# Turning half of a tile by DMA instead of TensorE, with token halves and a value load in two parts

## The chip, the cores and the metric

One core of one Trainium2 chip. The metric is device microseconds of one execution. Kernels are compared only within the same rounds. The profile is one execution, and its span (first to last instruction) is some 2 us under the time of the run.

## The reference

```python
kv = einsum('bhsd,bhse->bhde', k, v)            # 8 batches, 8 heads, 576 tokens, 64 wide
out = einsum('bhsd,bhde->bhse', q, kv)
out = out / sqrt(mean(out*out, -1) + 1e-6) * g_norm
x = out.transpose(0, 2, 1, 3).reshape(4608, 512)
xn = x / sqrt(mean(x*x, -1) + 1e-6) * rms_g     # then a gated feed-forward layer
g = xn @ w_gate                                 # 512 -> 1536
return (g * sigmoid(g) * (xn @ w_val)) @ w_out  # 1536 -> 512
```

## The kernel before

The kernel works through batches of 512 tokens (the 64 left over of each batch make a ninth). While TensorE runs the feed-forward of batch n, the other engines prepare batch n+1 and DMA loads n+2. A feed-forward has 12 *units*, each the gate and value products of 128 columns, and then 4 *down products*. The weights stand still in the array and the tokens move, so the normalised rows must first be turned: tokens along the free dimension (`xnt`). From batch 2 on DMA turns them. Batch 1 is turned by TensorE, four groups of four matmuls against an identity (the profile merges them into two of eight), and copied out of PSUM:

```python
def to_rows(x, n, c, ps, engine):
    for j in range(NS):
        PE.matmul(ps[:, j, :], lhsT=x[:, 2 * j : 2 * j + 2, :], rhs=identity, is_transpose=True, ...)
    cast(engine, xnts[n][:, :, 128 * c : 128 * c + 128], ps)
...
def load_batch(b):                    # queries, keys, values of one batch on the sync queue
    load_q(b)
    for name in ("k", "v"):
        alloc_kv(b, name)
        load_kv(b, name, nc.sync)
...
xs = [F.scale(c, F.outa[c]) for c in range(4)]     # batch 1's rows, VectorE
alloc_q(2)
for i in range(T):
    cast_q(2, i, SC if i < 2 else DVE)
for c in range(T):
    atts[2].q_rows(c)                 # batch 2's queries turned by DMA, sync queue
down_part(1, 8, 12)
f_x(0, xs[0], SC)                     # to_rows through TensorE
f_x(1, xs[1], SC)
down_part(2, 8, 12)
f_x(2, xs[2], DVE)
f_x(3, xs[3], DVE)
down_part(3, 8, 12)
for c in range(T):
    ffn.down_out(c)                   # batch 0's output, stored on the sync queue
```

Then the units of batch 1, with the work for batches 2 and 3 hung on them as steps:

```python
def up(self, j):                      # one unit: 8 matmuls of 512 tokens
    ...
def up_pair(self, i, lo, banks=None): # two units, 256 tokens: 16 matmuls of 256 tokens
    ...
steps[0] += [cast_kv(2, "v", i, GP) for i in (0, 1)]     # n == 1, cut
steps[1] += [cast_kv(2, "v", i, DVE) for i in (2, 3)]
steps[2] += [a.kv_products, a.kv_copy]                   # L289: key-value products of batch 2
steps[4] += [a.o_products]                               # L329: query products
...
for c in range(T):
    steps[13].append(lambda b=b, c=c: atts[b].q_rows(c)) # query turns of batch n + 2
```

Every engine takes its instructions in order, so a TensorE instruction that waits holds back all that follow (in the trace after, products of L289 waited 0.68 us until 60.06, and the pair of units behind them began only at 60.83).

## Time and profile before

| | before |
|---|---|
| time, median of the first 3 runs | 318.66 us (318.55 to 318.67) |
| span in the profile | 316.9 us |
| TensorE busy | 97% |
| VectorE, ScalarE busy | 57%, 56% |
| 16 KB instruction packets on queue 8 | 18 |

Read it from TensorE: where its row has no hole, only its own work counts. The lines of this are in the prediction below.

### The profile page before, as it was taken

What the parts mean: (1) busy time and instruction counts of PE and PEld (TensorE: products, weight loads), DVE (VectorE), ACT (ScalarE), POOL (GpSimd) and SP (SyncE); (2) the same over time, 40 slices, a digit from 0 to 9 for tenths busy, and PEclk for the clock granted to TensorE, in tenths of its full rate; (3) what the DMA queues carried; (4) which work ended last, traced back from release to release, by engine and by line L of the source; (5) the groups of instructions that cost most, each with busy time, mean ns of one, the idle gap of its engine ahead of it and who ended that gap; (6) DMA issues with size and microseconds to landing.
All of it is one profiled execution on the core that took longest, in us unless ns stands there. A gap on an engine that the chain in (4) does not pass through costs nothing.

```text
span 316.9 us, 6002 instructions
## 1 busy us (share of the span) xinstructions
PE 307.4 (97%) x2334; PEld 150.1 (47%) x2371; DVE 180.4 (57%) x377; ACT 176.5 (56%) x326; POOL 22.7 (7%) x48
## 2 busy tenths in 40 slices
PE   7899999999999999999999999999999999999995
PEld 3585455444444444444444444444444444444443
DVE  3676658679339913992289327941795079504310
ACT  3677458385667565746683668376844274233321
POOL 2364351100000000000000000000000000000000
PEclk9999999999999999999999999999999999999999
DMA  7999999587479157906790589838003710330014
GB/s 264 378 387 387 375 374 337 122 229 269 117 173 375 41 146 191 360 2 133 186 375 4 116 167 220 330 73 188 8 0 66 153 48 3 63 135 3 0 33 100
DMA packets 60316, 54.95 MB, mean 173 GB/s; under 512 B 36348, under 2 KB 44800, under 8 KB 60288
## 3 DMA queue, kind: packets, MB, share of 16 engines
q1 hardware_dynamic: 59776, 53.85, 56.6%
q10 hardware_dynamic: 448, 0.72, 0.7%
q8 instruction: 18, 0.29, 0.4%
q14 instruction: 10, 0.08, 0.1%
q0 software_dynamic: 64, 0.00, 0.0%
HBM read 37.75 MB, written 9.44 MB: 149 GB/s over the span
## 4 chain that ended last, share of the span: by engine, by line
PE 90%; DMA 5%; another core or an unknown queue 1%; issue 1%; SPq 1%; POOL 1%; DVE 0%; ACT 0%
PE v_ps L497 29%; PE g_ps L497 28%; PE o_ps L549 26%; DMA st<-in_moe_w_val_dram 3%; DMA st<-in_k_dram 2%; PE att_ps L289 2%; PE g_ps L549 1%; PE v_ps L549 1%; DMA out_dram<-o_sb 1%; PE att_ps L329 1%; PE o_ps L514 1%; POOL wv_sb L194 1%; PE o_ps L329 0%; PE att_ps L265 0%
## 5 line engine op out<-in xcount | busy, mean ns | idle before, releaser
L503 DVE TENSOR_TENSOR h_sb<-silu,v_ps 128x512 bf16<-128x512 bf16 x104 | 71.2, 684 | 100.1 <-ACT silu L502 68.5
L497 PE MATMUL v_ps<-xnt,wv_sb 128*128 128x512 bf16 x409 | 106.2, 379 | 0.7
L497 PE MATMUL g_ps<-xnt,wg_sb 128*128 128x512 bf16 x398 | 104.6, 379 | 0.7
L502 ACT ACTIVATE silu<-g_ps 128x512 bf16<-128x512 f32 x104 | 62.1, 597 | 70.2 <-PE g_ps L497 57.4
L549 PE MATMUL o_ps<-wo_sb,h_sb 128*128 128x512 bf16 x386 | 86.8, 379 | 0.4
L497 PEld LDWEIGHTS <-wv_sb 128*128 128x128 bf16 x416 | 40.7, 98 | 49.1
L549 PEld LDWEIGHTS <-h_sb 128*128 128x128 bf16 x420 | 40.6, 98 | 47.6 <-issue 0.4
L497 PEld LDWEIGHTS <-wg_sb 128*128 128x128 bf16 x416 | 39.5, 98 | 46.4
L105 ACT COPY o_sb<-o_ps 128x512 f32<-128x512 f32 (+1 forms) x34 | 19.6, 581 | 40.2 <-PE o_ps L549 36.6
L105 ACT CAST vb<-st 128x576 bf16<-128x576 f32 (+1 forms) x26 | 16.1, 662 | 3.7 <-DMA st<-in_v_dram 3.7
L376 DVE TENSOR_TENSOR xna<-outa,s1y 128x512 bf16<-128x512 bf16 x28 | 17.9, 684 | 0.0
L105 ACT CAST qb<-st 128x512 bf16<-128x512 f32 (+1 forms) x30 | 16.2, 602 | 2.3 <-DMA st<-in_q_dram 2.1
L359 DVE TENSOR_REDUCE ssq<-sqt 128x16 f32<-128x1024 bf16 x14 | 17.1, 1220 | 0.5
L359 DVE TENSOR_REDUCE ssq<-sq 128x16 f32<-128x1024 bf16 x14 | 17.1, 1220 | 0.5
L105 ACT CAST kb<-st 128x576 bf16<-128x576 f32 x20 | 12.5, 673 | 0.0
L344 ACT ACTIVATE sq<-att_ps 128x512 bf16<-128x512 f32 x14 | 7.6, 594 | 4.3 <-PE att_ps L329 3.6
L358 DVE TENSOR_TENSOR sq<-sq,gsq 128x512 bf16<-128x512 bf16 x14 | 5.9, 422 | 4.9 <-ACT sq L344 4.9
L107 DVE CAST kb<-st 128x576 bf16<-128x576 f32 x12 | 6.0, 518 | 4.2 <-DMA st<-in_k_dram 4.2
L649 PE MATMUL att_ps<-kv_all 128*128 128x512 bf16 (+1 forms) x21 | 7.1, 461 | 1.2 <-DVE sel L637 1.2
L107 POOL CAST wo_sb<-st 128x512 bf16<-128x512 f32 x12 | 7.3, 635 | 7.4 <-DMA st<-in_moe_w_out_dram 7.4
L344 ACT ACTIVATE sqt<-o_ps 128x512 bf16<-128x512 f32 x14 | 7.6, 597 | 0.0
L350 ACT CAST outa<-o_ps 128x512 bf16<-128x512 f32 x14 | 7.5, 591 | 0.0
(153 smaller groups left out, 182.1 us busy)
## 6 DMA issues: line engine op xcount, KB each, us to landing
st<-in_k_dram SPq DMA_DIRECT2D x7, 1152.0 KB, 10.1
st<-in_v_dram SPq DMA_DIRECT2D x7, 1152.0 KB, 11.7
out_dram<-o_sb SPq DMA_DIRECT2D x14, 512.0 KB, 3.0
st<-in_q_dram SPq DMA_DIRECT2D x6, 1024.0 KB, 6.7
st<-in_moe_w_out_dram SPq DMA_DIRECT2D x6, 512.0 KB, 10.4
st<-in_moe_w_gate_dram SPq DMA_DIRECT2D x4, 512.0 KB, 9.0
st<-in_moe_w_val_dram SPq DMA_DIRECT2D x4, 512.0 KB, 10.9
out_dram<-o_sb SPq DMA_DIRECT2D x14, 128.0 KB, 2.4
```

The lines of the kernel that those rows point to most:

```text
L105: engine.copy(out=dst, in_=src)
L107: engine.tensor_copy(out=dst, in_=src)
L289: PE.matmul(self.kv_ps[x][to, a, :], lhsT=kb[rows, 2 * a + x, c, :], rhs=vb[rows, 2 * a + x, c, :], start=(a == 0 and c == 0), stop=(a == ...
L344: SC.activation(out=self.in_place(self.sq[i][:, 0], g), in_=bank, func=ACT.Square)
L350: SC.copy(out=self.in_place(rows, g), in_=bank)
L359: DVE.reduce_sum(out=self.ssq[:, c], in_=sq, axis=AX.X)
L376: DVE.tensor_tensor(out=self.xna[c], in0=self.outa[c], in1=self.alpha[:, c, :].to_broadcast([128, H, D]), op=OP.mult)
L497: PE.matmul(ps, lhsT=wt[:, s, j * 128 : (j + 1) * 128], rhs=x[:, s, :], start=(s == 0), stop=(s == NS - 1),)
L502: SC.activation(out=silu, in_=g_ps, func=ACT.Silu)
L503: DVE.tensor_tensor(out=self.h[:, j, :], in0=silu, in1=v_ps, op=OP.mult)
L549: PE.matmul(self.o_ps[c], lhsT=self.h[:, j, c * 128 : (c + 1) * 128], rhs=wo_sb[:, j, :], start=(j == 0), stop=(j == NF - 1),)
L649: PE.matmul(ps[:, 0:w], lhsT=warm_sb[:, 0:128], rhs=warm_sb[:, 0:w], start=True, stop=True, skip_group_check=True)
```

## The change

Its intent: take the turns of token columns 2 and 3 off TensorE (8 matmuls and 2 copies) and give them to DMA. They land later than TensorE's would have, so the first four units run in halves: two pairs on the first 256 tokens, then two pairs on the rest. And so that the turns are not held up behind batch 2's values, half of those values is loaded after them.

```diff
-    def load_batch(b):
+    def load_batch(b, first=slice(0, NS)):
         load_q(b)
-        for name in ("k", "v"):
+        for name, js in (("k", slice(0, NS)), ("v", first)):
             alloc_kv(b, name)
-            load_kv(b, name, nc.sync)
+            load_kv(b, name, nc.sync, js)
...
-    load_batch(2)
+    load_batch(2, slice(0, 2))
...
     atts = {b: Att(b) for b in range(2, B + 1)}
+    for c in (2, 3):
+        nc.sync.dma_start_transpose(
+            out=xnts[1][:, :, 128 * c : 128 * c + 128], in_=xs[c].rearrange("p h d -> p (h d)")
+        )
+    load_kv(2, "v", nc.sync, slice(2, 4))
     for c in range(T):
         atts[2].q_rows(c)
...
-    f_x(2, xs[2], DVE)
-    f_x(3, xs[3], DVE)
...
-            if unit < NF:
+            if n == 1 and unit < 4:
+                i, lo = unit % 2, 256 * (unit // 2)
+                ffn.gate_pair(i, lo, ffn.up_pair(i, lo))
+            elif unit < NF:
                 ffn.up(unit)
```

## The prediction

> **What bounds the kernel now.** I read the page's table of busy shares first, then the chain of work that ended last, then the stretch that the change touches. The page says which engine to count on:
>
> ```profile
> PE 307.4 (97%) x2334; PEld 150.1 (47%) x2371; DVE 180.4 (57%) x377; ACT 176.5 (56%) x326; POOL 22.7 (7%) x48
> PE 90%; DMA 5%; another core or an unknown queue 1%; issue 1%; SPq 1%; POOL 1%; DVE 0%; ACT 0%
> ```
>
> The second line is the chain by engine. TensorE is busy for 97% of the span and carries 90% of the chain; the 5% of DMA is the opening load of batch 0 and the last store. VectorE and ScalarE work for little more than half of the span. So a change is worth what it takes off TensorE's own row of work, or adds to it as a wait, and hardly anything else.
>
> The change lies between the last down products of batch 0 and the first units of batch 1. The chain cut to 50 to 61 us (start, duration, what) shows it piece by piece:
>
> ```profile
> 50.28 1.73 PE o_ps L549 x8
> 52.00 0.45 PE att_ps L265 x8
> 52.45 0.86 PE g_ps L549 x4
> 53.31 0.46 PE att_ps L265 x8
> 53.77 0.86 PE v_ps L549 x4
> 54.63 0.22 PE g_ps L497
> 54.85 0.05 issue
> ...
> 58.95 0.86 PE v_ps L497 x4
> 59.81 0.71 PE att_ps L289 x72
> ```
>
> There is no hole: each piece starts where the one before ended. The two groups of L265 are the turns of batch 1's normalised rows through TensorE: eight small matmuls for token columns 0 and 1, eight for columns 2 and 3. From 54.63 on the units of batch 1 run, 1.73 us each (0.86 gate, 0.86 value), and at 59.81, after the third unit, stand the key-value products of batch 2.
>
> What the sync queue and VectorE do in these microseconds, from the timeline of each:
>
> ```profile
> 53.69 5.23 SPq L303 DMA_TRANSPOSE qt<-qb  x4
> 59.03 6.57 SPq L569 DMA_DIRECT2D out_dram<-o_sb  x8
> ```
> ```profile
> 52.19 0.68 DVE L478 TENSOR_TENSOR xna<-outa,F1y 128x512 bf16<-128x512 bf16 x1
> 52.79 0.75 DVE L107 CAST qb<-st 128x512 bf16<-128x512 f32 x2
> 53.58 0.76 DVE L107 COPY xnt<-att_ps 128x512 bf16<-128x512 bf16 x2
> ...
> 58.20 0.69 DVE L503 TENSOR_TENSOR h_sb<-silu,v_ps 128x512 bf16<-128x512 bf16 x1
> 58.80 0.82 DVE L107 CAST vb<-st 128x576 bf16<-128x576 f32 x2
> ```
>
> The last of the four scaled rows is ready at 52.87. The second copy out of PSUM ends at 54.34, 0.29 us before TensorE's first unit. The casts of batch 2's values for heads' groups 2 and 3 end at 59.62, 0.19 us before the products that read them. That second margin is thin, and the change touches it.
>
> **What the Trainium skill says.** "TensorE: Matmul & The Clock Gate", Part 4: PE-mode transpose, gives about 275 ns for one transpose in a kernel's context, and a copy out of PSUM after it. The trace has 216 to 219 ns as the duration of one, but the chain charges 0.46 us for eight, because they are pipelined; I use 0.46. The same page, Back-to-back issue gap, has 262 cycles for 256 columns and 518 for 512 (109 and 216 ns at its 2.4 GHz), so halving costs almost nothing provided that the weight load fits under the shorter matmul. The trace agrees: L514, batch 0's units in halves, has groups of 8 in 0.87 us (0.109 each), L497 has 4 in 0.86, and a weight load takes 98 ns, under 109. "DMA: Bandwidth & Descriptors", Queues, rings and completion order: descriptors of one queue are consumed in ring order on each DMA engine. So a turn issued behind a load waits for that load's packets. The trace has the first of the four query turns, issued at 53.69 behind the tail of the value load, at 2.9 us to landing, the rest at 2.5. "Perfetto Trace Analysis", DMA Instruction, HWDGE: the shown time of a DMA instruction is descriptor generation, not movement. Here one turn holds the sync queue for 1.27 us and lands 2.5 us after its start, so four in a row are paced by issue.
>
> **The change part by part.**
>
> (a) *Removed from TensorE:* the second group of L265, 0.46 us in the chain. Removed from VectorE: two copies of about 0.42 us; VectorE has room, so this counts for nothing. First unit: 54.63 - 0.46 = 54.17.
>
> (b) *Added to TensorE by the halves:* four units of 8 matmuls of 512 columns (4 x 1.73 = 6.91 us) become 64 matmuls of 256 columns: 64 x 0.1085 = 6.94. Cost 0.03 us. ScalarE and VectorE still do 4 activations and 4 products, each of 2 x 256 columns, the size of before.
>
> (c) *The two turns on the sync queue.* The third scaled row is ready about 52.25, the fourth at 52.87; add about 0.14 us for the wait (79.90 against 79.76 for the same hand-over in the next batch). First turn: issued 52.39, off the queue 53.65; second: 53.65 to 54.92. With 2.5 us to landing, and up to 0.4 more for packets ahead of them, the second lands at 56.15 to 56.55. With the halves, TensorE needs token columns 2 and 3 only after two pairs, at 54.17 + 2 x 1.735 = 57.64. More than 1 us to spare: these turns are hidden.
>
> (d) *The value load in two.* Before, the load's packets (2304 bytes) flow at full rate until about 53.8, stragglers to 55.4, and it lands at 56.0 to 56.2. Half of 1152 KB taken out is 576 KB, at about 380 GB/s (page, GB/s row) 1.5 us: first half down at about 54.5, before its user needs it, and the ring is nearly clear when the turns arrive. The second half is issued when the turns are off the queue, at about 54.95. Packets of loads issued into an empty ring start some 1.2 us after (59.03 issue, 60.2 first store packet). So 56.15 + 1.55 = 57.7 for the last packet, and some 0.5 to 1 us of receipt and stragglers: landing at 58.2 to 58.7.
>
> (e) *The products that wait for it.* VectorE's casts follow unit 1's product, which comes 0.44 us earlier than before: free at about 58.4. Casts take 0.82 to 0.90, so they end at 59.3 to 59.6; TensorE finishes its third unit at 54.17 + 3 x 1.735 = 59.38 and needs some 0.1 us after the cast. Wait: 0.05 to 0.35 us, my middle is 0.2.
>
> (f) *Later on the queue.* Query turns: from about 55.45, last landing at 55.45 + 3 x 1.27 + 2.5 = 61.8; their matmuls stand at about 63.6. Stores and the next batch's loads move back by 1.6 us; the next batch's first cast stands at 76.5 and its load was issued at 65.69 and took some 7 us. All keep their slack.
>
> Sum: -0.46 + 0.03 + 0.20 = -0.23 us. As TensorE runs without a hole to the end, a shift here passes to the end: 318.66 - 0.23 = 318.4.
>
> **The rivals.**
>
> *The wait replaces the turns' time.* If the second value half lands at 59.0 or later (slow DMA engines lag, or the query turns behind it interleave), casts end after 59.9 and TensorE waits over 0.5 us: time back at 318.7 or, at 59.5, 319.2. For it: the thin margin of 0.19 us before, and a load that now starts after two turns. Against: the load is only 576 KB in a nearly empty ring.
>
> *The full gain.* If the half lands by 58.3, the wait is nothing and the time is 318.66 - 0.43 = 318.2. For it: my landing estimate has its early edge there.
>
> *Coarse waiting.* If the first unit's matmuls wait for both turns, not for their own half of the tile, they start at 56.2 to 56.6, some 2 us late: 320.3. Against: batch 0 already starts its units on the first 256 tokens while the rest are being turned.
>
> *TensorE becomes bound by weight loads in the halves.* 64 loads of 98 ns are 6.27 us, under 6.94. It would show as over 0.12 us a matmul; the trace's L514 speaks against it.
>
> **Range and chances.** The terms run from -0.43 (no wait) to about +0.2 (a wait of 0.65); three runs of before spread over 0.12 us. That gives 318.1 to 318.9, widened to 317.9 to 319.0 for what I left out. Two per cent is 6.4 us: no term is near it, even coarse waiting is 1.7 us. So "within 2%" is almost certain.
>
> **What would show it.** (a) One group of L265 left in the chain, and the first unit at about 54.2. (b) Groups of 8 half matmuls at 0.87 us each. (c) Two more turns on the sync queue from about 52.4; no hole in TensorE's row before the third pair. (d, e) The value load's second half landing at 58.2 to 58.7; a hole of 0.05 to 0.35 us before the products of L289. (f) No wait at the query products. The prediction is wrong if that hole is over 0.6 us, if the turns land after 57.6, or if a later load, moved back, opens a hole in the next batch.

## The result, and the profile after

The changed kernel took 320.24 us (median of 6 fast runs, 319.97 to 320.9), the kernel before 318.75 us (6 fast runs, 318.55 to 319.48). The ratio is 1.0045, 95% interval 1.0031 to 1.0059. A ratio here is the mean time of one kernel's fast runs over that of the other's of the same rounds, so not quite the ratio of the medians quoted. Within 2%, as foretold; but 1.5 us slower instead of 0.2 us faster, and outside the range.

The page of the changed kernel, busy shares and the chain by engine:

```profile
PE 307.9 (97%) x2359; PEld 152.9 (48%) x2395; DVE 179.3 (56%) x375; ACT 176.3 (55%) x326; POOL 22.7 (7%) x48
PE 84%; DMA 8%; DVE 2%; SPq 2%; issue 1%; another core or an unknown queue 1%; POOL 1%; ACT 0%; DVEq 0%
```

The busy share did not move, but TensorE's share of the chain fell from 90% to 84%. That alone does not show a new wait: e9 below, which has none here, stands at 85%, because its chain goes through loads in the opening. What TensorE itself waited for, in total us, times, longest:

```profile
PE o_ps L329 <- DMA qt<-qb: 0.7, 1, 0.7
PE att_ps L671 <- ACT qb L105: 0.7, 1, 0.7
PE att_ps L289 <- DVE vb L107: 0.7, 1, 0.7
```

The middle line is in the opening, and was there before (0.9). The other two are new. The chain of the changed kernel from 50 to 61 us (this trace runs 0.45 us ahead of that of before: the first scaled row is taken up at 49.86 against 50.31; the operation itself starts 0.06 us later):

```profile
53.84 1.13 SPq L968
54.97 0.05 issue
55.03 4.50 DMA st<-in_v_dram
59.52 0.02 issue
59.55 0.04 DVE vb L107
59.58 0.34 issue
59.92 0.46 DVE vb L107
60.38 0.04 issue
60.43 0.47 PE att_ps L289 x34
```

The chain has left TensorE. It goes through the second half of the values (issued at 55.03, landed 59.52), VectorE's two casts of it, and only then comes back to TensorE, in the middle of the key-value products. The sync queue and VectorE in the same stretch:

```profile
51.85 3.12 SPq L968 DMA_TRANSPOSE xnt<-xna  x2
55.03 0.58 SPq L120 DMA_DIRECT2D st<-in_v_dram  x1
55.78 5.11 SPq L303 DMA_TRANSPOSE qt<-qb  x4
```
```profile
59.55 0.83 DVE L107 CAST vb<-st 128x576 bf16<-128x576 f32 x2 [1.53 <-DMA st<-in_v_dram]
```

VectorE stood idle for 1.53 us until the load had landed. Before, it went straight from unit 1's product to these casts, at 58.80.

The second new wait comes one batch later. The chain there:

```profile
90.56 4.23 DMA qt<-qb
94.80 0.05 issue
94.84 0.29 PE o_ps L329 x8
```

The last of batch 3's four query turns took 4.23 us to land, where 2.5 is usual. Before, there was no wait at the same place:

```profile
93.20 0.34 PE att_ps L329 x16
93.54 0.23 PE o_ps L329 x16
```

**Three measures that do not depend on the opening.** The opening varies between runs by more than the change is worth, so I measure in each trace (a) how long TensorE takes from the end of the work before the products of L289 to their end, (b) the same for the query products of L329 in batch 3, (c) the stretch from when the first scaled row of batch 1 (the first L478) is taken up to the last instruction. Each is of one profiled execution. All three are worked out from the starts and ends of the instructions in the trace.

| run | (a) L289 | (b) L329 | (c) scaled row to end | (c) minus that of before |
|---|---|---|---|---|
| before | 0.71 | 0.57 | 266.63 | |
| after | 1.93 | 1.49 | 268.27 | +1.64 |
| e1 values whole | 0.71 | 0.57 | 266.21 | -0.42 |
| e2 halves only | 0.71 | 1.30 | 267.45 | +0.82 |
| e3 before, 48 instructions more | 0.70 | 1.69 | 267.89 | +1.26 |
| e5 values whole, earlier query turns | 0.71 | 0.57 | 266.15 | -0.48 |
| e6 after, earlier query turns | 1.37 | 0.57 | 266.97 | +0.34 |
| e7 three quarters ahead | 0.70 | 1.48 | 267.15 | +0.52 |
| e8 = e1 again | 0.71 | 1.31 | 266.99 | +0.36 |
| e9 = e5 again | 0.71 | 0.57 | 266.19 | -0.44 |
| e10 before, earlier query turns | 0.71 | 0.57 | 266.67 | +0.04 |
| e11 after again | 1.18 | 1.62 | 267.63 | +1.00 |

For after: (a) grew by 1.22, (b) by 0.92, together 2.14; less the 0.46 of the turns that makes 1.68, against 1.64 measured. For e11: 0.47 + 1.05 - 0.46 = 1.06 against 1.00. So two waits account for the loss, and the saving is there beneath them.

### The profile page after: what moved, and what is told of

Same layout as the page of the kernel before. It is cut to its first block, busy times and chain, and to the rows that moved or that the text cites. A ratio compares the mean times of both kernels' runs of the same rounds, so it can differ in the third digit from the quotient of the medians.

```text
span 318.1 us, 6055 instructions
## 1 busy us (share of the span) xinstructions
PE 307.9 (97%) x2359; PEld 152.9 (48%) x2395; DVE 179.3 (56%) x375; ACT 176.3 (55%) x326; POOL 22.7 (7%) x48
## 4 chain that ended last, share of the span: by engine, by line
PE 84%; DMA 8%; DVE 2%; SPq 2%; issue 1%; another core or an unknown queue 1%; POOL 1%; ACT 0%; DVEq 0%
PE v_ps L497 27%; PE g_ps L497 26%; PE o_ps L549 25%; DMA st<-in_moe_w_val_dram 3%; DMA st<-in_k_dram 2%; DMA st<-in_v_dram 1%; DMA qt<-qb 1%; PE att_ps L289 1%; SPq L303 1%; DVE xna L478 1%; DMA out_dram<-o_sb 1%; PE o_ps L514 1%; PE g_ps L514 1%; POOL wv_sb L194 1%
## 5 line engine op out<-in xcount | busy, mean ns | idle before, releaser
L503 DVE TENSOR_TENSOR h_sb<-silu,v_ps 128x512 bf16<-128x512 bf16 x100 | 68.4, 684 | 98.1 <-ACT silu L502 68.3
L497 PE MATMUL v_ps<-xnt,wv_sb 128*128 128x512 bf16 x393 | 102.0, 379 | 0.6
L497 PE MATMUL g_ps<-xnt,wg_sb 128*128 128x512 bf16 x383 | 100.6, 379 | 0.6
L502 ACT ACTIVATE silu<-g_ps 128x512 bf16<-128x512 f32 x100 | 59.7, 597 | 68.4 <-PE g_ps L497 55.5
L497 PEld LDWEIGHTS <-wv_sb 128*128 128x128 bf16 x400 | 39.1, 98 | 47.2
L497 PEld LDWEIGHTS <-wg_sb 128*128 128x128 bf16 x400 | 38.1, 98 | 44.5
L105 ACT CAST kv_all<-att_ps 64x128 bf16<-64x128 f32 x14 | 3.6, 259 | 7.2 <-PE att_ps L289 7.1
```

The costliest lines, as they stand in the source:

```text
L105: engine.copy(out=dst, in_=src)
L497: PE.matmul(ps, lhsT=wt[:, s, j * 128 : (j + 1) * 128], rhs=x[:, s, :], start=(s == 0), stop=(s == NS - 1),)
L502: SC.activation(out=silu, in_=g_ps, func=ACT.Silu)
L503: DVE.tensor_tensor(out=self.h[:, j, :], in0=silu, in1=v_ps, op=OP.mult)
```

## The experiments

The theory: first, the second half of the values comes too late for L289; second, a fetch of TensorE's own instructions slows the last query turn of batch 3 (the trace shows a 16 KB packet of the kind "instruction" on queue 8 at 92.44 us, while that turn is in flight, and 15 of its 16 arrivals are in by 93.04 but the sixteenth at 94.80). The rivals: the turns themselves are late; the turns behind the load slow it; the second wait is just the sync queue pushed back.

**e1, values whole again**

```diff
-    load_batch(2, slice(0, 2))
+    load_batch(2)
...
-    load_kv(2, "v", nc.sync, slice(2, 4))
```

> The changed kernel with batch 2's values loaded whole, ahead of the two turns, as before; turns and token halves stay. Theory (TensorE lost 1.4 us because the second half of the values was issued at 55.0 and landed at 59.5): the values land near 56, the wait before the products of L289 goes, the turns land near 56.6 against a need at 57.6, so 1.4 us less than the changed kernel, about 318.8; if the late last query turn of batch 3 (0.7 us) also stays. Rival (the turns need the shorter load ahead of them, as the change's author took it): the turns come behind the whole load, land after 57.6 and the third pair of token halves waits 0.5 us or more; 319.5 or more.

Measured: 319.65 us (6 runs, 318.35 to 321.49) against 319.31 (11 runs, 318.74 to 319.93) of before, ratio 1.0015, interval 0.9991 to 1.0038: not to be told apart. This chip spread the kernel before over 1.2 us in 11 runs (the runs of the result above spread over 0.9 in 6), about as much as the effects looked for. The profile is clear, though: the two turns land at 56.28 and 56.67 behind the whole load, no unit waits, (a) is back at 0.71 and (c) is 0.42 us under before. The rival falls: the turns did not need the load cut. That profile also lacked the second wait, which the theory had left open.

**e8, the same kernel again**

> e1 again, beside e5, because its profile had no wait while most of its timed runs were slower. Theory: the fetch lands within 0.2 us of the last query turn's landing, so some runs pay the wait at L329 and some not: fastest run 0.4 us under before's fastest, slower ones up to 0.9 us over. Rival: noise of that chip alone, the same ratio as e5.

Measured: 319.68 us (6 runs, 319.12 to 320.51) against 319.31 of before, ratio 1.0016, interval 1.0001 to 1.0032. This time the profile has the wait at L329 (the last turn landed at 94.12 instead of some 92.6) and (c) is +0.36. So one kernel has it in one profile and not in another. Its fastest run was not under that of before (318.74), a miss.

**e2, halves alone**

```diff
 # the kernel before, with only this of the change
-            if unit < NF:
+            if n == 1 and unit < 4:
+                i, lo = unit % 2, 256 * (unit // 2)
+                ffn.gate_pair(i, lo, ffn.up_pair(i, lo))
+            elif unit < NF:
```

> The kernel before with the four units in token halves alone; turns through TensorE, values whole. Cost of the halves themselves by the chain: 64 x 0.1085 against 32 x 0.216, 0.03 us. Theory of the second wait (a 16 KB fetch of TensorE's instructions occupies one DMA engine just when the last query turn of batch 3 is in flight): this kernel has 64 more TensorE instructions than before, 16 more than the changed one, so the fetch comes at about the same place and the wait of up to 0.7 us at the products of L329 near 94 us appears here too: 318.8 to 319.4. Rival (that wait comes from turns and stores pushed back on the sync queue): nothing is pushed back here, no wait, 318.7.

Measured: 319.92 us (6 runs, 319.56 to 321.37) against 319.31, ratio 1.0026, interval 1.0008 to 1.0044. The median is over the span that I gave; the profiled run's opening was 1.4 us longer than before's (first scaled row at 51.68). Nothing of the values or the sync queue differs from before here, and still:

```profile
PE o_ps L329 <- DMA qt<-qb: 0.6, 1, 0.6
```

(b) grew by 0.73 and (c) by 0.82, so the halves themselves cost 0.09 at most. The rival that needs a pushed-back queue falls.

**e3, the kernel before with more TensorE instructions and nothing else**

```diff
-    warm(warm_ps, 9)
+    warm(warm_ps, 33, 140)
```

> The kernel before with its first 9 warm-up matmuls of 512 columns as 33 of 140: the same columns in the idle opening, 48 more TensorE instructions, as many as the changed kernel has; nothing else. Theory of the fetch: the fetch moves earlier by 48 instructions and falls into the flight of batch 3's last query turn; one of its 16 arrivals comes some 1.8 us after the others, TensorE waits about 0.7 us before L329 near 94 us; time 0.5 to 0.8 us over before. Rival (pushed-back queue): no wait there, time of before within 0.2 us.

Measured: 320.05 us (6 runs, 318.82 to 320.63) against 319.31, ratio 1.0017, interval 0.9999 to 1.0035. The chain and TensorE's waits in its profile:

```profile
89.93 4.44 DMA qt<-qb
94.36 0.05 issue
94.41 0.29 PE o_ps L329 x8
```
```profile
PE o_ps L329 <- DMA qt<-qb: 0.9, 1, 0.9
```

The interval of the times still holds no change; the profile carries the reading. The wait is there in a kernel that differs from before only in its warm-up at the very start, 33 small matmuls for 9 large ones. So more TensorE instructions ahead are enough to bring it, with nothing else moved (one profile; e2 is a second). Where the fetch fell, from the packets and arrivals in the traces of all runs:

| run | instruction packet starts | 15th arrival of the last turn | 16th arrival | late by |
|---|---|---|---|---|
| before | 93.52 | 92.55 | 92.56 | 0.0 |
| after | 92.44 | 93.04 | 94.80 | 1.8 |
| e2 | 93.56 | 94.08 | 95.62 | 1.5 |
| e3 | 92.38 | 92.41 | 94.37 | 2.0 |
| e4 | 96.01 | 96.54 | 98.46 | 1.9 |
| e7 | 91.44 | 92.05 | 93.80 | 1.7 |
| e8 | 92.01 | 92.60 | 94.12 | 1.5 |
| e11 | 92.49 | 93.10 | 94.98 | 1.9 |
| e1 | 92.04 | 92.18 | 92.19 | 0.0 |
| e6 | 92.15 | 92.21 | 92.22 | 0.0 |
| e5 | 93.34 | 91.54 | 91.55 | 0.0 |
| e9 | 92.89 | 91.79 | 91.80 | 0.0 |
| e10 | 93.50 | 91.56 | 91.57 | 0.0 |

Where the packet starts after the turn has landed, nothing is late; where it starts half a microsecond before the 15th arrival, one arrival is late. Close to the end it goes either way (e3 late at 0.03 us, e1 and e6 not at 0.14 and 0.06). The packets in the traces tell why. The turn's packets end with 32 of 4 bytes. In all seven late rows thirty of these start in time, and the last two start within 0.02 us of the end of the instruction packet (after: 93.75 and 93.76 against 93.77), 0.7 to 1.2 us behind the other thirty. In e1 and e6 all 32 had started (the last at 91.87 and 91.89) before the instruction packet did; in e3 two had not. So the late share stood behind the instruction packet.

That the packet is TensorE's instruction stream is inferred, from two counts. The pages have 18 such packets in the two kernels with 2371 weight loads of TensorE (before and e10), and 19 in all those with 2395 or 2403:

```profile
q8 instruction: 18, 0.29, 0.4%
q8 instruction: 19, 0.31, 0.4%
```

And the packets keep step with TensorE: the eighth of them starts when 967 weight loads have begun in before and e10, and 973 to 975 in every other run, though the times differ by several us (107.2 to 112.8).

**e4, nothing behind the second half of the values**

```diff
-        cast_q(2, i, SC if i < 2 else DVE)
+        if i < 3:
+            cast_q(2, i, SC if i < 2 else DVE)
...
-    for c in range(T):
-        atts[2].q_rows(c)
...
+            steps[1] += [lambda: cast_q(2, 3, DVE)]
+            steps[1] += [lambda c=c: atts[2].q_rows(c) for c in range(T)]
 # and batch 0's stores after these (cut)
```

> The changed kernel, but nothing follows the second half of the values on the sync queue for some 2.5 us: batch 2's query turns wait for a cast placed after the second pair, and batch 0's stores come after them. Its time is not of interest (the query products may wait). Theory (a load starts slowly by itself: its first 1.5 us move a quarter of the later rate): the second half still takes 4.3 to 4.5 us from issue to landing. Rival (the query turns issued straight behind it slow it): it takes 3.4 us or less.

Measured (one look, 323.91 us, as the query products now wait): 55.13 to 59.18, 4.05 us, between the two. The turns behind the load cost 0.2 to 0.45 us (4.26, 4.32 and 4.49 in e11, e6 and after); most of the lateness is the load's own.

**e7, a quarter behind instead of a half**

```diff
-    load_batch(2, slice(0, 2))
+    load_batch(2, slice(0, 3))
-    load_kv(2, "v", nc.sync, slice(2, 4))
+    load_kv(2, "v", nc.sync, slice(3, 4))
```

> The changed kernel with three quarters of the values ahead of the turns and one quarter (288 KB) behind. Question: how much of the 4.49 us from issue to landing of the 576 KB is fixed. My prediction took 2.0 us fixed and 1.5 us of transfer at full rate, so 2.7 to 2.9 us for 288 KB and no wait at L289. Theory of the slow start (the first 2 us move only some 300 KB whatever the size): 3.5 us or more, and a wait at L289 of 0.3 to 0.8 us stays.

Measured (one look): 3.07 us from issue to landing, and no wait at L289. My theory of a fixed slow start of 3.5 us or more is wrong. Against the same queue order with 576 KB (4.26 to 4.49), the second 288 KB cost 1.2 to 1.4 us, where 380 GB/s would make it 0.78; what does not scale is 1.65 to 1.9 us, about what the prediction allowed. So it is the transfer that was mis-sized. The packets of the load show it directly: the 576 KB ran for 2.49 to 2.85 us in e4, e11, e6 and after, the 288 KB here for 1.52, which is 190 to 240 GB/s; ahead of them stand 1.18 to 1.23 us from issue to the first packet, and after them 0.35 to 0.41 to the landing. And they show how: counted from its first packet, the load of after moved 56 KB in the first 0.5 us, then 63, 83, 196 and 162, while the loads from 50 to 52 us moved 182 to 191 KB in each such slice. e4 has the same climb (52, 83, 180, 202) with nothing behind the load, so the turns behind do not make it. Why a load climbs slowly I did not settle.

**e6, the changed kernel with batch 3's query turns one unit sooner**

```diff
-                steps[13].append(lambda b=b, c=c: atts[b].q_rows(c))
+                steps[12 if n == 1 else 13].append(lambda b=b, c=c: atts[b].q_rows(c))
```

> The changed kernel with the earlier query turns of batch 3 alone; the values stay in two loads. Theory: the wait at L329 goes or shrinks below 0.3 us, the one at L289 stays; the stretch from the first scaled row to the end falls from 268.3 by some 1.0 us to 267.2; time 0.6 us over before. Rival (the wait at L329 follows from the later stores and loads and moves with them): about the changed kernel, 1.5 us over before.

Measured: 319.29 us (5 runs, 319.2 to 319.5) against 319.31, ratio 1.0002, interval 0.999 to 1.0014. (b) is back at 0.57, (a) is 1.37, (c) 266.97, 1.3 us under after (whose profile is of other rounds). The time that I expected, 0.6 us over before, did not show. The second wait goes alone, with the first left in place: they are two causes.

**e5, both waits taken away: e1 with the edit of e6**

> The changed kernel with both waits taken away: values whole as in e1, and batch 3's query turns issued one unit sooner, ahead of batch 1's first store, so that the last turn has landed about 0.6 us earlier and the instruction fetch finds the store in flight. Theory: no wait at L289 nor at L329; from the first scaled row of batch 1 to the end 266.2 us in the profile against 266.6 before; time 0.4 us under before of the same rounds (ratio 0.9987). Rival (something else than these two waits holds the changed kernel back): time of before or over.

Measured: 318.62 us (6 runs, 318.48 to 320.36), ratio 0.9995, interval 0.9975 to 1.0015. In the profile (a) and (b) are as before and (c) is 0.48 us shorter, as expected; the timed gain is not shown.

**e9, e5 again; e10, the control; e11, after again** (one other chip, same rounds)

> e5 again, because its interval (0.9975 to 1.0015) was too wide for a gain of 0.4 us. Theory: no wait at L289 or L329, stretch from the first scaled row of batch 1 to the end 266.2 us against 266.6 before; ratio 0.9985 to 0.9990. Rival (the gain is lost in other places that the profile of one run does not show): ratio 1.000 or more.

> Control: the kernel before with the earlier query turns of batch 3 alone. Theory: there was no wait to remove, so the time of before, ratio 0.9995 to 1.0005. Rival (e5 gains by the earlier query turns and not by the turns taken off TensorE): as e5.

> The changed kernel unaltered, on the chip of e9 and e10, for comparison: both waits, product stretches of about 1.9 us (L289) and up to 1.5 us (L329), ratio 1.003 to 1.006.

Measured, with the kernel before at 318.98 us (9 runs, 318.76 to 319.39): e9 318.81 (318.71 to 319.0), ratio 0.9995, interval 0.9983 to 1.0008; e10 318.87 (318.67 to 319.19), ratio 0.9997, interval 0.9984 to 1.0009; e11 320.32 (319.87 to 320.44), ratio 1.0038, interval 1.0024 to 1.0052. The chain of e9, to set beside that of before in the prediction:

```profile
52.10 0.45 PE att_ps L265 x8
52.54 0.86 PE g_ps L549 x4
53.41 0.86 PE v_ps L549 x4
54.27 0.87 PE g_ps L514 x8
...
58.64 0.87 PE v_ps L514 x8
59.51 0.71 PE att_ps L289 x72
60.22 0.98 PE g_ps L514 x8
```

One group of L265 is gone, the halves stand at 0.87 us each, and no hole is left. The profile has the stretch (c) 0.44 us under before, and the control at +0.04. The times do not confirm it: the ratio I expected was 0.9985 to 0.9990, and 0.9995 with that interval holds both a gain of 0.4 us and none. So the repaired kernel is 1.5 us faster than the changed one on the same chip (318.81 against 320.32), and against the kernel before a gain is seen in the profiles only.

## Why the prediction was wrong

Two steps failed: (d), the landing of the second half of the values, and (f), that everything later keeps its slack. The saving in (a) stood up, in the profiles, and lies beneath both waits.

- **(a) and (b), the turns and the halves: right.** The second group of L265 left the chain, a half costs 0.87 us per eight matmuls, and with both waits gone the stretch is 0.42 to 0.48 us shorter against 0.43 foretold.
- **(c), the turns on the queue: right in what matters.** They landed at 54.83 and 56.19, before the third pair. But the first one held the sync queue for 1.82 us, not 1.27 (1.31 to 1.81 in the eight other runs that have it). That put the second half of the values, counted from the first scaled row, at 5.17 us instead of 4.64; in e11, at 4.65, the estimate held. Why one run has it and another not stays open. (One reading was off: the 0.14 us added for the hand-over took 79.76 as the end of a scaled row that ends at 79.84 in the trace. That did not matter: the first turn was issued 1.99 us after the first scaled row was taken up, 2.08 foretold.)
- **(d), the landing: the mis-sized term.** I allowed 3.25 to 3.75 us from issue to landing; it was 4.26 to 4.49 (4.05 with nothing behind it), because I let the load run at the 380 GB/s of mid-stream. In after its packets ran from 56.26 to 59.11, 2.85 us where I had 1.55, or 207 GB/s. The other two terms were not short: the first packet came 1.23 us after issue (1.2 foretold), the landing 0.41 after the last packet (0.5 to 1). Of the lateness in after, 0.53 us comes from the issue in (c) and the rest from here; in e11 it comes from here alone. In after, landing came at 9.66 us from the first scaled row, foretold 7.9 to 8.4.
- **(e), the wait: right mechanism, wrong size.** The prediction put it at 0.05 to 0.35 us; it was 1.22 in after and 0.47 in e11. The rival "the wait replaces the turns' time" is what happened, and the thin margin of 0.19 us was the right place to look.
- **(f), "All keep their slack": failed.** I checked the issue times of later transfers, not what else uses the DMA engines. The change adds 64 TensorE instructions and removes 16; that moved an instruction fetch into the last query turn of batch 3, which before had landed 0.6 us ahead of the query products, and cost 0.92 to 1.05 us. With this wait alone the time would have been near 319.2 (318.66 - 0.43 + 0.92); with e11's wait at L289 alone near 318.7, inside the range. The sum had no term for it.
- **The rivals "coarse waiting" and "bound by weight loads"** did not occur.

## What to carry to other kernels

When TensorE has no hole, work taken off it pays in full only if nothing that it will wait for moves later: list the thin margins near the change, and size the landing of a moved load from loads of like size that start on an idle ring, not from the rate in mid-stream. Adding instructions was not free here even where they took no more of TensorE's time: it shifted when instructions were fetched, and a fetch held up one share of a transfer with little slack. If a wait turns up far from an edit, pad the old kernel with as many instructions and see whether it comes too; and look whether the late share of the transfer starts where an instruction packet ends.

## What the Trainium skill lacked or had wrong

- "DMA: Bandwidth & Descriptors", Queues, rings and completion order, gives queue row 14 to refills, and "Runtime: NRT & Kernel Launch", Instruction fetch mechanics, calls the cost of crossing a 16 KiB block of instructions mostly hidden. Neither says what a fetch does to a transfer on another queue. Here 16 KB packets of the kind "instruction" ran on queue 8, 18 or 19 per execution, each 0.9 to 1.7 us long in the stretch studied, and in the seven late rows of the table above one arrival of a turn came 1.5 to 2.0 us after its other fifteen, and TensorE waited 0.6 to 0.9 us for it.
- "DMA: Bandwidth & Descriptors", Anatomy of one DMA, fits 2.0 us plus bytes over 436 GB/s, for the GpSimd path. It has no fit for the sync queue, from which 576 KB took 4.05 to 4.49 us here and 288 KB 3.07, where that fit would give 3.35 and 2.68.
- "TensorE: Matmul & The Clock Gate", Back-to-back issue gap, gives about 131 ns per 512-column matmul as the sustained spacing in a real kernel. The trace has 0.216 us (4 in 0.86), which is the page's other figure, for an isolated gap (216 ns).
- The same page, Part 4: PE-mode transpose, counts about 275 ns for one transpose; eight in a row took 0.45 to 0.46 us in the chain, 57 ns each.
